# Two-sided attention decode: A's output weights loaded between the two halves of the last A pair's V, and the slots of the last three loads exchanged

## The chip, the cores and the metric

The kernel runs on one core of one Trainium2 chip. The metric is the device time of one execution in microseconds. Before the change it is 831.22 us, the median of 3 runs (830.82 to 831.3). Times in the trace are counted from the start of the profiled execution's span.

## What is computed

Two attention decodes of one token, A and B, with 32 heads of 128 each and no sharing of K and V between heads. Side A looks at all 16384 cached positions, side B at the last 4096. For each side:

```python
q = (x @ wq)                                  # 512 -> 32 heads x 128
scores = einsum("bhqd,bhkd->bhqk", q, k) * (Dh ** -0.5)
p = softmax(scores)
o = einsum("bhqk,bhkd->bhqd", p, v)
out = o.reshape(B, Sq, Hq * Dh) @ wo          # 4096 -> 512
# B: k, v are cut to the last W = 4096 positions
return concatenate([a, b], axis=-1)
```

Nearly all of the data is K and V: 268 MB for A, 67 MB for B. Each of the four weight matrices (A's and B's `wq` and `wo`) has 4096 KB. Every element is read once.

## The kernel before

**Steps.** The work is cut into 20 steps T = 0..19 (lines 88 to 97). Sixteen are pairs of A heads, four are groups of eight B heads (T = 0, 7, 13, 19). So T = 18 is the last A pair, and T = 19 is the last step, B's. Each step has two halves u = 0, 1: for A the two halves of the positions of one pair of heads, for B two groups of four heads. A loop over x = 2T + u (line 400) runs all halves in order, and `tc.manual_schedule()` (line 374) keeps each engine's instructions in the order in which the program writes them.

**A half.** VectorE multiplies the half's K by q (`scores_prod`, L194), adds up over the head dimension in four halvings (`scores_tree`, L201) and one reduction (L207), and takes the maximum (L212). TensorE and VectorE bring the maximum of each head together (L214, L219, L223, L226), ScalarE makes the exponentials and spreads them by head (`soft`, L231 to L253). TensorE multiplies the probabilities with V (`pv`, L275, 32 matmuls of 128x512 for a half). ScalarE scales and evicts (L291), and eight small matmuls (L306) and a copy (L310) turn the result into columns of O.

**What lies one step behind.** V of step T is loaded and multiplied while step T + 1 is scored. At x = 38, the first half of step 19, the program issues `pv(17, 1)`, then the load of V(18, 1), then `pv(18, 0)`. At x = 39 come `pv(18, 1)` and the loads for the end. Here V(T, u) is the half u of step T's V.

**Slots.** K tiles live in a ring of two K slots of 8192 KB each (`kslot`, tag `kring`), V halves and the `wq` matrices in a ring of two V slots of 4096 KB each (`vslot`, tag `vring`). A load into a slot waits until the slot's last readers are done. V(18, 0) and V(19, 0) use one V slot, V(18, 1) and V(19, 1) the other. After step 18's scores, its K slot is free; before the change it takes A's `wo` in one half and B's `wo` in the other (`W`, lines 409 and 424).

**Queue.** All loads of K, V and weights are issued by SyncE, in program order, on one queue. A wait in front of one load holds back all the loads behind it. The order of the loads at the end, before the change: K of step 19 (two halves), V(17, 1), V(18, 0), V(18, 1), V(19, 0), A's `wo`, V(19, 1), B's `wo` in five pieces (16, 8, 4, 2 and 2 of 32 rows per partition).

**The end.** After the loop, TensorE's program order is: the last maximum and sums, `pv(19, 0)` (L275), its columns (L306), A's permutation and output projection (`permute_o` L327 and L332, `project_out_columns` L345, 128 matmuls), the transposition of A's output (L363), then `pv_columns` for V(19, 1) (L317, 128 matmuls), B's permutation, B's output projection (L345, 128 matmuls in five pieces, each of which waits for its piece of B's `wo`), and B's output (L357, L363, L367, store L368).

Of the kernel before, what the change touches and what calls it, by code (L numbers as in the profile page):

```python
# [16 lines left out]
HQ, DH = 32, 128  # L17
CH = 128
# [7 lines left out]
def kernel(  # L26
# [34 lines left out]
    def kslot(name):  # L61
        return kring.tile([P, 2 * CH, DH], BF16, tag="kring", name=name)

    def vslot(name):
        return vring.tile([P, CH, DH], BF16, tag="vring", name=name)
# [7 lines left out]
    A, B = _Side(), _Side()  # L73
# [22 lines left out]
    NT = len(steps)  # L96
    assert na == HQ // 2 and nb == HQ // 8

    K, V = {}, {}

    def b_window(cache, g):
        return cache[0, 4 * g : 4 * g + 4, SkB - WB : SkB, :].rearrange("h (i l) d -> i h (l d)", l=CH)

    def a_pair(cache, g):
        return cache[0, 2 * g : 2 * g + 2, :, :].rearrange("h (i l) d -> (h i) l d", l=2 * CH)

    def new_k(T):
        K[T] = kslot("kt")

    def load_k(T, u=None):  # L110
        s, g = steps[T]
        if s is A:
            nc.sync.dma_start(
                out=K[T][:, :, :].rearrange("p l d -> p (l d)"),
                in_=a_pair(A_k_cache, g).rearrange("p l d -> p (l d)"),
            )
        else:
            for v in (0, 1) if u is None else (u,):
                nc.sync.dma_start(
                    out=K[T][:, v * CH : (v + 1) * CH, :].rearrange("p l d -> p (l d)"),  # L120
                    in_=b_window(B_k_cache, 2 * g + v),
                )

    def load_v(T, u):
        s, g = steps[T]
        V[T, u] = vslot("vt")
        if s is A:
            src = a_pair(A_v_cache, g)[:, u * CH : (u + 1) * CH, :].rearrange("p l d -> p (l d)")
        else:
            src = b_window(B_v_cache, 2 * g + u)  # L130
        nc.sync.dma_start(out=V[T, u][:, :, :].rearrange("p l d -> p (l d)"), in_=src)

    def load_wq(s):
        s.wq_t = vslot("wqt")
        nc.sync.dma_start(
            out=s.wq_t[:, :, :].rearrange("p a b -> p (a b)").rearrange("p (c f) -> p c f", c=KC),
            in_=s.wq.rearrange("(p c) f -> p c f", c=KC),
        )

    def load_wo(s, W, u, pieces):  # L140
        s.wo_t = W[:, u * CH : (u + 1) * CH, :].rearrange("p a b -> p (a b)").rearrange("p (r f) -> p r f", r=HQ)
        src = s.wo.rearrange("(p r) f -> p r f", r=HQ)
        r = 0
        for n in pieces:
            nc.sync.dma_start(out=s.wo_t[:, r : r + n, :], in_=src[:, r : r + n, :])  # L145
            r += n

    def make_masks(s):
        nc.vector.tensor_reduce(out=s.mask[:, :], in_=by_head(s, identf[:, :]), axis=AX.X, op=ALU.add)
        nc.vector.tensor_copy(s.rows[:, :, :], s.mask[:, :].unsqueeze(2).broadcast_to([P, s.nh, 4]))  # L150

    def spread_x(s, flat):
        s.xb = flat[:, 0 : s.nh * KC * P].rearrange("p (h c m) -> p h c m", h=s.nh, c=KC)
        nc.vector.memset(s.xb, 0.0)
        for j in range(s.nh):
            dst = s.xb[:, j, :, :]
            if s is A:
                dst = dst.rearrange("p c (h i) -> p c h i", h=s.nh)[:, :, j, :]
            else:
                dst = dst.rearrange("p c (i h) -> p c i h", h=s.nh)[:, :, :, j]  # L160
            nc.vector.tensor_copy(dst, s.xT[:, :].unsqueeze(2).broadcast_to([P, KC, P // s.nh]))  # L161

    def project_q(s):
        wq = s.wq_t[:, :, :].rearrange("p a b -> p (a b)").rearrange(
            "p (c g h d) -> p c h g d", c=KC, h=s.nh, d=DH
        )
        for g in range(0, HQ // s.nh, 4):
            qp = ps_t.tile([P, 4, DH], F32, tag="tp", name="qp")
            n = KC * s.nh
            for k in range(n):  # L170
                c, j = divmod(k, s.nh)
                nc.tensor.matmul(  # L172
                    qp[:, :, :], lhsT=s.xb[:, j, c, :], rhs=wq[:, c, j, g : g + 4, :],
                    start=(k == 0), stop=(k == n - 1),
                )
            nc.scalar.copy(s.q[:, g : g + 4, :], qp[:, :, :])
# [13 lines left out]
    def scores_prod(T, u):  # L190
        s, g = steps[T]
        k = K[T][:, u * CH : (u + 1) * CH, :]
        j = g if s is A else 2 * g + u
        nc.vector.tensor_tensor(out=k, in0=k, in1=s.q[:, j : j + 1, :].broadcast_to([P, CH, DH]), op=ALU.mult)  # L194
# [63 lines left out]
    def recip(un):  # L258
        un.r = small.tile([P, 4], F32, tag="r", name="r")
        if un.last:  # L260
            nc.vector.reciprocal(un.r[:, 0 : un.s.nh], un.sm[:, 136 : 136 + un.s.nh])
        else:
            nc.vector.reciprocal(un.r[0 : un.rows, 0:1], un.sm[0 : un.rows, 136:137])  # L263
# [35 lines left out]
    def columns():  # L299
        while evicted:  # L300
            un = evicted.pop(0)
            s, n = un.s, un.rows
            oc = ps_s.tile([P, 4], F32, tag="sp", name="oc")
            sel = identf[0:n, 0:n].rearrange("k (h c) -> k c h", c=4)
            for j in range(4):
                nc.tensor.matmul(  # L306
                    oc[:, 0 : s.nh], lhsT=un.osb[0:n, j * P : (j + 1) * P], rhs=sel[:, j, :],
                    start=(j == 0), stop=(j == 3),
                )
            nc.scalar.copy(s.O[:, un.col : un.col + s.nh], oc[:, 0 : s.nh])  # L310
# [62 lines left out]
    wo_pieces = (16, 8, 4, 2, 2)  # L373
    with tc.manual_schedule():
        for s in (B, A):
            nc.scalar.dma_start(out=s.xT[:, :], in_=s.x[0, 0, :].rearrange("(p c) -> p c", c=KC))
        scratch = kslot("scratch")
        new_k(0)
        load_wq(B)
        load_k(0, 0)  # L380
        load_wq(A)
        load_k(0, 1)
        make_identity(nc, identf[:, :])
        nc.vector.memset(one_f[:, :], 1.0)
        nc.vector.memset(ones_col[:, :], 1.0)
        nc.vector.tensor_copy(ident[:, :], identf[:, :])
        spread_x(B, scratch[:, :, :].rearrange("p a b -> p (a b)"))
        for s in (B, A):
            make_masks(s)
        nc.vector.memset(pick[:, :], 0.0)  # L390
        nc.vector.tensor_copy(
            pick[:, 4 : 4 + P].rearrange("h (m k) -> h m k", k=4)[:, :, 0], identf[0:HQ, 0:HQ]
        )
        spread_x(A, one.tile([P, 2 * KC * P], BF16, tag="o4", name="xbA")[:, :])
        project_q(B)
        project_q(A)
        new_k(1)
        load_k(1)
        done = None
        for x in range(2 * NT):  # L400
            T, u = divmod(x, 2)
            if u == 0 and T >= 1:
                load_v(T - 1, 0)
                if T + 1 < NT:
                    new_k(T + 1)
                    load_k(T + 1)
            if x == 2 * NT - 1:
                load_v(T, 0)
                W = kslot("wot")
                load_wo(A, W, 0, (HQ,))  # L410
            columns()
            scores_prod(T, u)
            if done is not None:
                max_all(done)
                soft(done)
            if u == 0 and T >= 1:
                if T >= 2:
                    pv(T - 2, 1)
                load_v(T - 1, 1)
                pv(T - 1, 0)  # L420
            if x == 2 * NT - 1:
                pv(T - 1, 1)
                load_v(T, 1)
                load_wo(B, W, 1, wo_pieces)
            nxt = scores_tree(T, u)
            if done is not None:
                recip(done)
            evict()
            done = nxt
            if done is not None:  # L430
                unit_max(done)
        columns()
        max_all(done)
        soft(done)
        recip(done)
        pv(NT - 1, 0)
        evict()
        columns()
        permute_o(A)
        project_out_columns(A, (HQ,))  # L440
        store_out(A)
        pv_columns(NT - 1, 1)
        permute_o(B)
        project_out_columns(B, wo_pieces)
        store_out(B)
# [30 lines left out]
```

## Time and profile before

| what | before |
| --- | --- |
| median of 3 runs | 831.22 us (830.82 to 831.3) |
| the profiled execution | 831.32 us |
| its span | 829.5 us |
| bytes read | 352.32 MB |
| VectorE busy | 761.0 us, 92% |
| TensorE matmul busy | 395.2 us, 48% |
| ScalarE busy | 67.8 us, 8% |

The span runs from the first to the last instruction of the trace. The rest of the execution's time, 1.8 us, lies around it. "PE" is TensorE's matmuls, "PEld" its weight loads, "DVE" VectorE, "ACT" ScalarE, and "SPq" what SyncE issues on its DMA queue. A row of a view by windows gives a stretch, the busy time and instruction count of each engine in it, the clock that TensorE was granted (1.00 is full speed), the mean busy share of the 16 DMA engines and the rate that they moved. A row of a timeline gives start, duration, engine, line, operation and names, a count, and in brackets how long the engine was idle before it and which event ended that. The time "to landing" of a load runs from its issue to the last event that reports its arrival.

### The profile page before, as it was taken

To read this page: it belongs to the slowest core of one execution; us is meant where nothing else is said; L and a number is where in the kernel's file an instruction comes from. 1 tells how busy PE (TensorE), PEld (TensorE's weight loads), DVE (VectorE), ACT (ScalarE), POOL (GpSimd) and SP (SyncE) were. 2 spreads that over 40 slices of the span, in tenths; PEclk is the share of its full clock that TensorE was granted. 3 is DMA by queue.
4 is the path that set the end of the run, shared out by engine and by line. 5 is a ranking of instruction groups with operands and counts; after the bars stand their busy time and mean duration, and the time that the engine had idled before them with its cause. 6 is when DMAs were issued, how large, how long until landed. Compare 5 with 4: busy or idle time off the path is not lost.

```text
span 829.5 us, 4817 instructions
## 1 busy us (share of the span) xinstructions
PE 395.2 (48%) x2012; PEld 172.7 (21%) x2012; DVE 761.0 (92%) x356; ACT 67.8 (8%) x196; POOL 0.7 (0%) x6
## 2 busy tenths in 40 slices
PE   3514062808163543637081725455362708082885
PEld 1102021303021211213030312122221303030344
DVE  1899999999999999999999999999999999999920
ACT  0111010101000011101010000011010101000120
POOL 0000000000000000000000000000000000000000
PEclk9756566758595867667585958576666758585895
DMA  9999999999999999999999999999999999999797
GB/s 379 430 430 437 433 458 411 453 408 432 435 427 430 437 455 411 450 412 448 416 444 417 440 425 431 450 416 450 416 441 420 444 417 443 425 433 433 331 431 305
DMA packets 10694, 352.64 MB, mean 425 GB/s; under 512 B 1456, under 2 KB 1456, under 8 KB 1840
## 3 DMA queue, kind: packets, MB, share of 16 engines
q1 hardware_dynamic: 10376, 352.33, 98.7%
q8 instruction: 16, 0.26, 0.1%
q10 hardware_dynamic: 296, 0.00, 0.0%
q14 instruction: 6, 0.05, 0.0%
HBM read 352.32 MB, written 0.00 MB: 425 GB/s over the span
## 4 chain that ended last, share of the span: by engine, by line
DVE 79%; DMA 17%; PE 2%; issue 1%; SPq 0%; ACT 0%; DVEq 0%; ACTq 0%
DVE kt L194 36%; DVE kt L201 35%; DMA kt<-in_A_k_cache_dram 10%; DVE sc L207 5%; DMA wot<-in_B_wo_dram 3%; DMA xTA<-in_A_x_dram 3%; PE o L275 2%; DMA vt<-in_A_v_cache_dram 1%; DVE m L212 1%; DVE Mr L223 1%; DVE M L219 0%; SPq L145 0%; DVE r L263 0%; ACT p L234 0%; PE sm L226 0%
## 5 line engine op out<-in xcount | busy, mean ns | idle before, releaser
L201 DVE TENSOR_TENSOR kt<-kt 128x8192 bf16<-128x8192 bf16 (+3 forms) x160 | 344.9, 2156 | 4.7
L275 PE MATMUL o<-vt,pm 128*8 128x512 bf16 (+1 forms) x1248 | 316.3, 420 | 2.5 <-DMA vt<-in_A_v_cache_dram 2.5
L194 DVE TENSOR_TENSOR kt<-kt,qA 128x16384 bf16<-128x16384 bf16 x32 | 277.5, 8672 | 3.0 <-DMA kt<-in_A_k_cache_dram 3.0
L275 PEld LDWEIGHTS <-pm 128*8 128x8 bf16 (+1 forms) x1248 | 116.2, 94 | 192.5 <-issue 65.1
L214 PE MATMUL sm<-identf,m 128*1 128x128 f32 x24 | 8.4, 350 | 196.7 <-DVE m L212 196.7
L226 PE MATMUL sm<-one_f,Mr 1*128 1x1 f32 x48 | 13.1, 340 | 176.7 <-DVE Mr L223 176.7
L194 DVE TENSOR_TENSOR kt<-kt,qB 128x16384 bf16<-128x16384 bf16 x8 | 69.5, 8681 | 0.0
L207 DVE TENSOR_REDUCE sc<-kt 128x128 f32<-128x1024 bf16 x40 | 48.8, 1220 | 2.9
L226 PEld LDWEIGHTS sm<-one_f,Mr 1*128 1x128 f32 x48 | 11.1, 285 | 183.1 <-DVE Mr L223 183.1
L214 PEld LDWEIGHTS sm<-identf,m 128*1 128x1 f32 x24 | 1.9, 79 | 200.1 <-issue 191.3
L231 ACT ACTIVATE bias<-sm 128x1 f32<-128x1 f32 x24 | 4.1, 171 | 386.8 <-PE sm L226 386.6
L291 ACT ACTIVATE o<-o,r 8x512 f32<-8x512 f32 (+1 forms) x23 | 15.6, 678 | 176.5 <-PE o L275 176.5
L306 PE MATMUL oc<-identf,o 8*128 8x2 f32 (+1 forms) x184 | 25.1, 254 | 3.7 <-ACT o L291 3.7
L306 PEld LDWEIGHTS oc<-identf,o 8*128 8x128 f32 (+1 forms) x184 | 23.1, 193 | 12.0 <-issue 6.5
L321 DVE TENSOR_TENSOR OB<-ocol,r 128x4 bf16<-128x4 f32 x1 | 0.2, 161 | 21.3 <-PE ocol L317 21.3
L172 PE MATMUL qp<-wqt,scratch 128*128 128x512 bf16 x32 | 9.1, 455 | 13.8 <-DVE scratch L161 13.8
L253 ACT ACTIVATE pm<-p,maskA 128x256 bf16<-128x256 bf16 x32 | 14.5, 500 | 0.5
L172 PE MATMUL qp<-wqt,xbA 128*128 128x512 bf16 x32 | 9.7, 475 | 10.2 <-DMA wqt<-in_A_wq_dram 10.2
L310 ACT CAST OA<-oc 128x2 bf16<-128x2 f32 x16 | 2.6, 160 | 109.9 <-PE oc L306 109.9
L234 ACT ACTIVATE p<-sc,bias 128x256 bf16<-128x256 f32 (+1 forms) x24 | 11.3, 472 | 0.8
L161 DVE COPY scratch<-xTB 128x128 bf16<-128x128 bf16 x4 | 0.7, 314 | 10.8 <-DMA xTB<-in_B_x_dram 10.8
L253 ACT ACTIVATE pm<-p,maskB 128x128 bf16<-128x128 bf16 x32 | 10.2, 389 | 0.2
(57 smaller groups left out, 81.5 us busy)
## 6 DMA issues: line engine op xcount, KB each, us to landing
vt<-in_A_v_cache_dram SPq DMA_DIRECT2D x32, 4096.0 KB, 26.8
kt<-in_B_k_cache_dram SPq DMA_DIRECT2D x8, 4096.0 KB, 30.6
vt<-in_B_v_cache_dram SPq DMA_DIRECT2D x8, 4096.0 KB, 29.2
wqt<-in_B_wq_dram SPq DMA_DIRECT2D x1, 4096.0 KB, 12.4
wqt<-in_A_wq_dram SPq DMA_DIRECT2D x1, 4096.0 KB, 31.1
wot<-in_A_wo_dram SPq DMA_DIRECT2D x1, 4096.0 KB
wot<-in_B_wo_dram SPq DMA_DIRECT2D x1, 2048.0 KB, 25.7
wot<-in_B_wo_dram SPq DMA_DIRECT2D x1, 1024.0 KB, 27.6
```

Of the source, the lines that this page charges most:

```text
L172: nc.tensor.matmul(qp[:, :, :], lhsT=s.xb[:, j, c, :], rhs=wq[:, c, j, g : g + 4, :], start=(k == 0), stop=(k == n - 1),)
L194: nc.vector.tensor_tensor(out=k, in0=k, in1=s.q[:, j : j + 1, :].broadcast_to([P, CH, DH]), op=ALU.mult)
L201: nc.vector.tensor_tensor(out=k[:, :, 0:w], in0=k[:, :, 0:w], in1=k[:, :, w : 2 * w], op=ALU.add)
L207: nc.vector.tensor_reduce(out=un.sc[:, c0 : c0 + CH], in_=k[:, :, 0:8], axis=AX.X, op=ALU.add)
L212: nc.vector.tensor_reduce(out=m[:, :], in_=un.sc[:, 0 : un.n], axis=AX.X, op=ALU.max)
L214: nc.tensor.transpose(un.sm[0:1, 0:P], m[:, :], identf[:, :])
L226: nc.tensor.matmul(un.sm[:, 128:129], lhsT=Mr[:, :], rhs=one_f[:, :], start=True, stop=True)
L234: nc.scalar.activation(out=p[:, 0 : un.n], in_=un.sc[:, 0 : un.n], func=ACT.Exp, scale=inv, bias=bias[:, :], accum_out=cs[:, :],)
L253: nc.scalar.activation(out=un.pm[:, :, j, :], in_=p[:, 0 : un.n].rearrange("p (i c) -> p i c", c=4), func=ACT.Copy, scale=s.mask[:, j : j ...
L275: nc.tensor.matmul(un.o[0 : un.rows, :], lhsT=un.pm[:, i0 + i, :, :].rearrange("p a b -> p (a b)"), rhs=V[T, u][:, 4 * i : 4 * i + 4, :], ...
L291: nc.scalar.activation(out=un.osb[0 : un.rows, :], in_=un.o[0 : un.rows, :], func=ACT.Copy, scale=un.r[0 : un.rows, 0:1],)
L306: nc.tensor.matmul(oc[:, 0 : s.nh], lhsT=un.osb[0:n, j * P : (j + 1) * P], rhs=sel[:, j, :], start=(j == 0), stop=(j == 3),)
```

## The change

Three edits, all about where and when the last four loads go.

1. A's `wo` is issued one half-step earlier, at x = 38 (2·NT − 2) in place of x = 39. In SyncE's order it now stands between V(18, 0) and V(18, 1), and it still goes into the first half of step 18's K slot.
2. V(19, 1) no longer takes a V slot, but the second half of that K slot, and is issued right behind V(19, 0), ahead of `pv(18, 1)` in the program.
3. B's `wo` takes the V slot that V(19, 1) had, the one that V(18, 1) was in, so its load waits for `pv(18, 1)`. `load_wo` takes a whole slot in place of a slot and a half's number.

The order of the loads after the change: K of step 19, V(17, 1), V(18, 0), A's `wo`, V(18, 1), V(19, 0), V(19, 1), B's `wo` in the same five pieces. The instructions of TensorE, VectorE and ScalarE and their order are the same as before.

```diff
-    def load_v(T, u):
+    def load_v(T, u, dst=None):
         s, g = steps[T]
-        V[T, u] = vslot("vt")
+        V[T, u] = vslot("vt") if dst is None else dst
...
-    def load_wo(s, W, u, pieces):
-        s.wo_t = W[:, u * CH : (u + 1) * CH, :].rearrange("p a b -> p (a b)").rearrange("p (r f) -> p r f", r=HQ)
+    def load_wo(s, W, pieces):
+        s.wo_t = W.rearrange("p a b -> p (a b)").rearrange("p (r f) -> p r f", r=HQ)
...
+            if x == 2 * NT - 2:
+                W = kslot("wot")
+                load_wo(A, W[:, 0:CH, :], (HQ,))
             if x == 2 * NT - 1:
                 load_v(T, 0)
-                W = kslot("wot")
-                load_wo(A, W, 0, (HQ,))
+                load_v(T, 1, W[:, CH : 2 * CH, :])
             columns()
...
             if x == 2 * NT - 1:
                 pv(T - 1, 1)
-                load_v(T, 1)
-                load_wo(B, W, 1, wo_pieces)
+                load_wo(B, vslot("wot")[:, :, :], wo_pieces)
```

## The prediction

> **What bounds the kernel now.** I read the page's bytes first, then the chain that ended last, then the last 60 us by timeline and by windows.
>
> ```profile
> HBM read 352.32 MB, written 0.00 MB: 425 GB/s over the span
> DVE 79%; DMA 17%; PE 2%; issue 1%; SPq 0%; ACT 0%; DVEq 0%; ACTq 0%
> ```
>
> The chain gives VectorE 79%, but the DMA engines show nines in almost all forty slices: the loads are one unbroken stream, and VectorE, 92% busy, keeps up with it. The change touches only the end, so what counts is what limits that stretch. The chain of waits, in order of time, has there:
>
> ```profile
> 763.84 9.46 PE o L275 x32
> 773.31 12.04 DMA vt<-in_A_v_cache_dram
> 785.39 8.98 PE o L275 x32
> ...
> 797.13 28.59 DMA wot<-in_B_wo_dram
> ```
>
> `pv(17, 1)` ends at 773.2 and frees a V slot; only then is V(18, 1) issued (773.31), and it lands 12.04 us later. At the very end the last piece of B's `wo` is what is waited for. Between the two the stream is unbroken. In front of it is a hole, as the windows around 773 show:
>
> ```profile
> 764.00:768.00 4.00, 4.00 (x11) 1.23 (x10) 3.97 (x2) 0.53 (x2) 0.00 (x0) 0.50 0.99 426
> 768.00:772.00 4.00, 4.00 (x18) 1.51 (x17) 3.83 (x5) 0.00 (x0) 0.00 (x0) 0.90 0.53 225
> 772.00:776.00 4.00, 4.00 (x20) 1.62 (x19) 4.00 (x4) 0.68 (x1) 0.00 (x0) 1.00 0.44 131
> 776.00:780.00 4.00, 4.00 (x20) 1.50 (x18) 4.00 (x1) 0.00 (x0) 0.00 (x0) 1.00 1.16 500
> ```
>
> The last column is the rate. Against the mean of 425 GB/s the second window lacks 200 and the third 294 GB/s, the fourth gives 75 back: 419 GB/s over 4 us, 1.7 MB or 3.9 us of the stream. This hole is what A's `wo` can fill. The question is who then sets the end, and for that TensorE's timeline from 785 counts:
>
> ```profile
> 785.39 8.98 PE L275 MATMUL o<-vt,pm 128*8 128x512 bf16 x32 [2.48 <-DMA vt<-in_A_v_cache_dram]
> ...
> 811.92 0.38 PE L363 MATMUL out_rows<-identf,cols 128*4 128x128 f32 x1 [0.25 <-ACT cols L361]
> 815.83 3.57 PE L317 MATMUL ocol<-pm,vt 128*128 128x4 bf16 x128 [3.54 <-DMA vt<-in_B_v_cache_dram]
> ...
> 820.83 1.85 PE L345 MATMUL out_cols<-OpB,wot 128*128 128x1 bf16 x64 [0.27 <-ACT OpB L336]
> 823.23 1.01 PE L345 MATMUL out_cols<-OpB,wot 128*128 128x1 bf16 x32 [0.56 <-DMA wot<-in_B_wo_dram]
> 824.51 1.00 PE L345 MATMUL out_cols<-OpB,wot 128*128 128x1 bf16 x24 [0.26 <-DMA wot<-in_B_wo_dram]
> 825.78 0.38 PE L345 MATMUL out_cols<-OpB,wot 128*128 128x1 bf16 x8 [0.27 <-DMA wot<-in_B_wo_dram]
> ```
>
> The brackets are the point. After `pv(18, 1)` TensorE waits for loads only 3.54 + 0.56 + 0.26 + 0.27 = 4.63 us in all. A second chain, TensorE's, runs that close behind the stream, and it starts when V(18, 1) lands.
>
> **A's wo ahead of V(18, 1).** Its slot is free when step 18's last reduction ends (VectorE, L207, 751.40 + 1.22 = 752.6), so it is issued there, long before the hole, and SyncE is held by nothing new. V(18, 1) is still issued at 773.31, since that waits for `pv(17, 1)`, but now behind A's `wo`.
>
> When does it land? From issue plus time to landing: the second half of step 19's K 714.5 + 39.2 = 753.7, V(17, 1) 735.47 + 27.9 = 763.4, V(18, 0) 742.38 + 30.7 = 773.1. So a full queue lands 4096 KB every 9.7 us, in order of issue. A's `wo` lands at 773.1 + 9.7 = 782.8, and V(18, 1) at **792.5**, which is 7.1 us later than 785.35 now. The hole gives back only 2.6 of the 9.7 us, because a load has landed when its slowest DMA engine is done: the busy share falls from about 768.5 on, but that engine goes on to 773. Bounds: if the lag were not carried on, the stream would follow the engines that end first, 768.5 + 2 × 9.7 = 788 and a little for arrival, so 789; if one engine is held up in this stretch, as between V(19, 0) (780.23 + 15.0 = 795.2) and V(19, 1) (794.41 + 21.4 = 815.8), which took 20.6 us for two loads in place of 19.4, 793.7. I take 792.5; two plain steps of 9.7 are the nearest rows.
>
> One rule can be weighed here. The row first: V(18, 1) into an empty queue took 12.04 us, while loads into a full one took about 28 to 31. The Trainium skill, "DMA: Bandwidth & Descriptors", section "Rules for kernel authors", advises to issue a DMA early and wait late, since the fixed cost then overlaps; its section on the anatomy of a DMA fits about 2.0 us plus bytes over 436 GB/s, 11.6 us here, near the row. By that rule the early `wo` hides some 2 us and the sum would be about 829. By the rows the early load, which nobody needs before 815, stands in an in-order queue ahead of one that TensorE is waiting for.
>
> **pv(18, 1).** It costs 8.98 us now, after a short idle of 2.48; `pv(17, 1)`, after a long one, costs 9.46; `pv(18, 0)`, warm from the start, 6.97. The granted clock is 0.50 at the start of each of the first two, and 1.00 later. It will now start after 9.6 us of idle. The longest cold start nearby: the 64 matmuls from 609.22 took 16.92 us, which less a warm half of 6.97 leaves 9.95. Idle time seems to add little beyond the first microseconds, so I take 9.2, between 8.98 and 9.46, with 7.0 and 10.0 as ends. It ends at 792.5 + 9.2 = 801.7.
>
> **From there to A's output.** The same instructions as now, 794.38 to 812.30, 17.92 us: maximum, sums, `pv(19, 0)`, columns, projection of A. V(19, 0) lands at 802.2, and `pv(19, 0)` would start at 797.85 + 7.3 = 805.2, so it waits for nothing. A's `wo` has long been there. End at 819.6.
>
> **V(19, 1) in the K slot.** It is issued right behind V(19, 0) at about 780.8, since the slot needs no further wait, and lands at 802.2 + 9.7 = 811.9 (now 815.8). Being early is worth nothing: TensorE comes to it at 819.6. So the wait of 3.54 us goes. `pv_columns` takes 3.57 us (granted clock 0.50 already, so it can't get slower by that), and from its end to B's projection are 820.83 - 819.40 = 1.43 us: 824.6.
>
> **B's wo in the V slot.** This adds a wait, for `pv(18, 1)`, until 801.7. Behind it in SyncE's queue is only the last store. The stream has work until 811.9, so the wait is hidden; five issues take 2.62 us. Without that cover it would cost up to the 12 us of a load into an empty queue. Landing: 811.9 + 9.9 (825.7 - 815.8 now) = 821.8, before TensorE comes to it at 824.6. So the waits between pieces go. The 128 matmuls then cost between 3.56 (A's, busy) and 4.24 (B's, busy, 1.85 + 1.01 + 1.00 + 0.38), A's with its gap 3.90; I take 3.8: 828.4 in place of 826.17.
>
> **The sum.** From the last of these matmuls to the end of the span are 829.5 - 826.17 = 3.4 us, unchanged: 831.8, so **+2.3 us**. The same by waits: V(18, 1) +7.15, `pv(18, 1)` +0.2, less 3.54 for V(19, 1), less 5.34 - 3.8 = 1.54 in B's projection: +2.3. The profiled execution took 831.32 us, 0.1 above the median of the runs: 831.3 + 2.3 = **833.6 us**, 0.29% slower. VectorE's work ends at 791.7 either way. What a measurement of this kernel can tell from no change is about 0.2%, 1.7 us.
>
> **Rivals.**
>
> 1. *The stream alone sets the end* (faster). Its last landing moves from 825.7 to 821.8, 3.9 us, giving 827.4. For it: the chain now ends in B's `wo` for 28.59 us. Against it: TensorE's chain has only 4.63 us of waits to give, and V(18, 1) comes 7.1 us later. It decides only where V(18, 1) lands before about 786. 5%.
> 2. *V(18, 1) comes 2 to 3.5 us earlier than I take* (no change): the lag of the slowest engine is made up while A's `wo` runs. Then it lands at 789 to 790.5, and the end is 831.3 + 2.3 - 3.5 to 831.3 + 2.3 - 2 = 830.1 to 831.6. For it: the mean engine is idle for 3.9 us, not 2.6. Against it: three loads in a row landed 9.7 us apart with the lag in place. 22%.
> 3. *TensorE's slow start takes longer* (slower still): `pv(18, 1)` at 10.0 us, and a delayed engine on top, 792.5 + 1.2: 831.3 + 2.3 + 0.8 + 1.2 = 835.6. For it: both have happened in this trace. Against it: not in the same stretch. 6%.
> 4. *The change does not reorder the stream*: A's `wo` is held by some wait until 773. Then V(18, 1) still follows it, with the hole back: landing at 785.35 + 9.7 = 795.1, worse by another 2.6 us, 836.2. Against it: the only reader of the slot is done at 752.6. 1%.
>
> **Numbers.** My forecast of 833.6 has 66%, between 832.9 and 835.5. With the rivals: slower by over 0.2% 0.72, within 0.2% 0.23, faster 0.05. The range of 831.2 to 835.6 takes in the upper part of rival 2 and the ends of the unknown terms, and leaves out rivals 1 and 4 and the lower part of rival 2.
>
> **What would show it.** Right: no hole near 773 in the windows; `pv(18, 1)` starts at about 792.5 on a wait for its V; `pv_columns` follows A's output transposition without a wait for a load; B's projection in one stretch; the chain of waits at the end all TensorE from 792 on. Wrong: `pv(18, 1)` before 790, or any wait for B's `wo` left, or a DMA link at the chain's end.
>
> A second rule stands by itself. The row is the granted clock, 0.50 for the first 3.9 us of `pv(18, 1)` now and for 5.1 us of `pv(17, 1)`. The Trainium skill, "TensorE: Matmul & The Clock Gate", Part 1, says that a cold array runs at half clock until a free-running window of about 3.4 us was busy throughout, so how long depends on where the first matmul falls. By the page `pv(18, 1)` would average 9.5 us and the sum be 833.9; by the rows it is 833.6.

## The result, and the profile after

The changed kernel takes 833.78 us, the median of 8 runs (833.3 to 836.83), against 831.03 of before (830.51 to 831.3) on the same chip. The ratio is 1.0045, with a 95% interval of 1.0029 to 1.0061: slower. The profiled execution took 833.46 us with a span of 831.7.

The eight runs fall into two groups, five from 833.3 to 834.1 and three from 836.7 to 836.8. The profiled execution is of the first group. The second group is taken up in the first experiment.

The windows around the old hole, of the changed kernel (the last column is the rate in GB/s, the one before it the busy share of the DMA engines):

```profile
768.00:772.00 4.00, 4.00 (x17) 1.45 (x15) 3.83 (x4) 0.00 (x0) 0.00 (x0) 0.81 1.01 434
772.00:776.00 4.00, 4.00 (x20) 1.66 (x19) 4.00 (x4) 0.68 (x1) 0.00 (x0) 1.00 1.03 438
```

The hole is gone: 434 and 438 GB/s where 225 and 131 stood. A's `wo` is issued at 752.70 and lands 30.2 us later, at 782.9. The chain of waits, in order of time, shows what that does:

```profile
773.70 18.88 DMA vt<-in_A_v_cache_dram
792.62 9.16 PE o L275 x32
...
805.31 7.02 PE o L275 x32
...
818.52 0.60 issue
...
824.75 3.57 PE out_cols L345 x128
```

V(18, 1) takes 18.88 us from issue to landing in place of 12.04. From there to the end no load appears in the chain any more; before, it ended in 28.59 us of waiting for B's `wo`. TensorE's timeline of the same profile:

```profile
792.62 9.14 PE L275 MATMUL o<-vt,pm 128*8 128x512 bf16 x32 [9.65 <-DMA vt<-in_A_v_cache_dram]
...
819.72 3.60 PE L317 MATMUL ocol<-pm,wot 128*128 128x4 bf16 x128
...
824.75 3.56 PE L345 MATMUL out_cols<-OpB,wot 128*128 128x1 bf16 x128 [0.27 <-ACT OpB L336]
```

One wait has grown from 2.48 to 9.65 us (ahead of `pv(18, 1)`), and those for V(19, 1) and for the pieces of B's `wo`, 4.63 us in all, are gone: `pv_columns` has no bracket, and B's projection is one stretch of 128 where it was four.

### The profile page after: what moved, and what is told of

The parts are those of the page before. It is cut to its first block, busy times and chain, and to the rows that moved or that the text cites. A ratio compares the mean times of both kernels' runs of the same rounds, so it can differ in the third digit from the quotient of the medians.

```text
span 831.7 us, 4818 instructions
## 1 busy us (share of the span) xinstructions
PE 394.2 (47%) x2012; PEld 171.9 (21%) x2012; DVE 761.0 (92%) x356; ACT 67.8 (8%) x196; POOL 0.7 (0%) x6
## 4 chain that ended last, share of the span: by engine, by line
DVE 79%; DMA 15%; PE 5%; issue 1%; ACT 1%; DVEq 0%; ACTq 0%
DVE kt L194 36%; DVE kt L201 35%; DMA kt<-in_A_k_cache_dram 10%; DVE sc L207 5%; PE o L275 3%; DMA xTA<-in_A_x_dram 3%; DMA vt<-in_A_v_cache_dram 2%; PE out_cols L345 1%; DVE m L212 1%; DVE Mr L223 1%; DVE M L219 0%; PE ocol L317 0%; PE oc L306 0%; ACT o L291 0%; DVE r L263 0%
## 5 line engine op out<-in xcount | busy, mean ns | idle before, releaser
L219 DVE TENSOR_REDUCE M<-sm 1x2 f32<-1x128 f32 (+1 forms) x24 | 6.5, 271 | 10.2 <-PE sm L214 10.2
## 6 DMA issues: line engine op xcount, KB each, us to landing
wot<-in_A_wo_dram SPq DMA_DIRECT2D x1, 4096.0 KB, 30.2
```

## The experiments

Each kernel ran in alternation with the kernel before on the same chip. Ratios are against those runs.

### The changed kernel again: what are the two groups?

No edit.

> The changed kernel unaltered. Its eight runs so far lie in two groups, 833.3 to 834.1 (five) and 836.7 to 836.8 (three), while the runs of before stay within 830.5 to 831.3. Theory (TensorE's chain after V(18, 1) sets the end): every run is 2.3 us or more above before, and what scatters is the chain's slow starts. Rival (one DMA engine is held up by up to 3 us in some executions): then before would scatter as much, since its end is a load. A run of the second group, if the profile catches one, shows which term grew: the landing of V(18, 1) (792.6 in the profile of after), pv(18, 1) (9.14) or pv(19, 0) (7.07).

Measured: 836.44 us (833.91 to 836.72, 5 runs), ratio 1.0054 (1.0040 to 1.0068). One run was in the first group, four in the second, and the profile caught one of these (836.41 us, span 834.6). The 24 runs of before spread from 830.13 to 832.07, evenly. TensorE's timeline of this slower execution:

```profile
792.76 9.62 PE L275 MATMUL o<-vt,pm 128*8 128x512 bf16 x32 [9.65 <-DMA vt<-in_A_v_cache_dram]
...
806.05 9.80 PE L275 MATMUL o<-vt,pm 128*16 128x512 bf16 x32
```

V(18, 1) is there at 792.76 in place of 792.62, so it is no load. `pv(18, 1)` costs 0.5 us more, and `pv(19, 0)` 9.80 us in place of 7.07. The windows of the two `pv` and of the stretch between them, first of this execution, then of the faster one of the first profile (the third column from the end is the granted clock):

```profile
792.76:802.38 9.62, 9.62 (x33) 3.26 (x32) 0.00 (x0) 0.00 (x0) 0.00 (x0) 0.73 1.01 436
802.38:806.05 3.67, 1.98 (x13) 1.69 (x13) 0.55 (x2) 2.37 (x9) 0.00 (x0) 0.83 0.99 429
806.05:815.85 9.80, 9.80 (x33) 3.39 (x32) 0.18 (x1) 0.60 (x3) 0.00 (x0) 0.72 0.95 404
```

```profile
792.62:801.76 9.14, 9.14 (x33) 3.17 (x32) 0.00 (x0) 0.00 (x0) 0.00 (x0) 0.77 1.00 430
801.76:805.24 3.48, 1.79 (x14) 1.50 (x14) 0.55 (x2) 2.17 (x8) 0.00 (x0) 1.00 1.03 443
805.24:812.31 7.07, 7.07 (x33) 2.80 (x32) 0.18 (x1) 0.80 (x3) 0.00 (x0) 1.00 0.96 413
```

Between the two `pv` TensorE is busy for about half of 3.5 us. In one execution the clock stays at 1.00 through that, in the other it drops, and the next 32 matmuls pay for it: 0.5 + 0.2 + 2.7 = 3.4 us with the slower sums, less the stall of 0.60 us ("issue" in the first profile's chain) that is absent here, comes close to the 2.9 between the spans.

### TensorE kept busy ahead of pv(18, 1)

```diff
             if x == 2 * NT - 1:
+                wm = ps_t.tile([16, 512], F32, tag="tp", name="wm")
+                for i in range(32):
+                    nc.tensor.matmul(
+                        wm[:, :], lhsT=ident[:, 0:16], rhs=A.q[:, 0:4, :], start=(i == 0), stop=(i == 31)
+                    )
                 pv(T - 1, 1)
```

> The changed kernel with 32 more matmuls of 16x512 on constant operands, written to a PSUM tile that nobody reads, put on TensorE just ahead of pv(18, 1), where it is idle for 9.65 us. They keep TensorE busy until V(18, 1) lands. Theory (the chain from V(18, 1)'s landing sets the end, and a slow start is one of its terms): V(18, 1) lands at 792.6 as before, pv(18, 1) falls from 9.14 to about 7.0, span 831.7 - 2.1 = 829.6, time about 831.3. If the group near 836.7 comes from slow starts in pv(18, 1), it disappears here. Rival (the end is set by the stream): no change, 833.5.

Measured: 833.53 us (831.76 to 833.64, 8 runs), ratio 1.0022 (1.0012 to 1.0032). TensorE's timeline of a run of 833.64:

```profile
792.39 7.07 PE L275 MATMUL o<-vt,pm 128*8 128x512 bf16 x32 [1.25 <-DMA vt<-in_A_v_cache_dram]
...
803.13 8.51 PE L275 MATMUL o<-vt,pm 128*16 128x512 bf16 x32
...
818.34 2.67 PE L317 MATMUL ocol<-pm,wot 128*128 128x4 bf16 x93
822.35 1.07 PE L317 MATMUL ocol<-pm,wot 128*128 128x4 bf16 x35 [1.34 <-issue]
```

`pv(18, 1)` costs 7.07 us, as expected, and the group near 836.7 is gone. Two runs only (831.76 and 832.0) come near the expected 831.3; the other six lie at 833.5 to 833.6. In the one of these that was profiled, the clock drops ahead of `pv(19, 0)` instead (8.51 us), and a stall of 1.34 us appears in `pv_columns`, after 93 of 128 matmuls, on nothing but "issue" (time in which the engine waits for nothing that the profile shows).

### The extra matmuls in the gap as well

```diff
+        fill(3)
         columns()
         max_all(done)
+        fill(5)
         soft(done)
```

`fill(n)` is the block of the last experiment with n matmuls; `fill(32)` stays ahead of `pv(18, 1)`.

> The changed kernel with the 32 extra matmuls ahead of pv(18, 1) and eight more between pv(18, 1) and pv(19, 0) (three ahead of the columns, five ahead of the sums), all into a PSUM tile that nobody reads. Theory (the two groups of runs differ by the clock in pv(19, 0), which drops in some executions since TensorE does little in the 3.7 us between the two): pv(18, 1) and pv(19, 0) both take about 7.1 us, and the runs are one group near 831.8 to 832.3, since at most 0.3 us of the extra matmuls is on the path. Rival (the groups come from the loads): two groups remain, about 3 us apart.

Measured: 832.24 us (831.77 to 833.63, 11 runs), ratio 1.0016 (1.0007 to 1.0025). Nine runs lie within 831.8 and 832.5, two at 833.6. The profile:

```profile
792.41 7.07 PE L275 MATMUL o<-vt,pm 128*8 128x512 bf16 x32 [1.04 <-DMA vt<-in_A_v_cache_dram]
...
803.06 7.07 PE L275 MATMUL o<-vt,pm 128*16 128x512 bf16 x32
...
816.87 2.45 PE L317 MATMUL ocol<-pm,wot 128*128 128x4 bf16 x85
820.30 1.28 PE L317 MATMUL ocol<-pm,wot 128*128 128x4 bf16 x43 [0.98 <-issue]
```

Both `pv` run at full clock, and the groups 3 us apart are gone. So the two groups are TensorE's clock. Even with both `pv` at full clock in the profile, the median is 1.0 us behind the runs of before (831.27); the profiled run (831.86) has a stall of 0.98 us in `pv_columns`. What the two runs at 833.6 are was not profiled.

### Half and a quarter of A's wo ahead

```diff
-                load_wo(A, W[:, 0:CH, :], (HQ,))
+                load_wo(A, W[:, 0:CH, :], (16,))
             if x == 2 * NT - 1:
                 load_v(T, 0)
+                load_wo(A, W[:, 0:CH, :], (HQ - 16,), 16)
                 load_v(T, 1, W[:, CH : 2 * CH, :])
```

The last argument is the first row. For the quarter it is 8 in place of 16.

> The changed kernel, but only half of A's wo (2048 KB) goes ahead of V(18, 1); the other half is issued behind V(19, 0). Slots as in the changed kernel. Theory (V(18, 1) is late by what stands ahead of it, less the 2.6 us of hole): V(18, 1) lands at 773.1 + 4.9 + 9.7 = 787.7, TensorE's chain then ends 4.9 us sooner than in the changed kernel, span 826.9, unless the stream ends it: its last landing is 821.8 in either case, which gives 825.6. So span about 827, time about 828.7, 2.4 us under before. Rival (the new slots and the wait of B's wo cost the time): as slow as the changed kernel, 833.5.

> As the kernel with half of A's wo ahead, but with a quarter (1024 KB). Theory: V(18, 1) lands at 773.1 + 2.4 + 9.7 = 785.2, as in before, so TensorE's chain is not late at all; the hole is nearly filled, and the stream ends at about 821.8 in place of 825.7, which sets the end: span about 825.7, time 827.4, 3.8 us under before (0.45%). Rival (filling the hole is worth nothing, since TensorE or VectorE bounds the end anyway): 831.

Measured: half 832.09 us (830.37 to 832.59, 11 runs), ratio 1.0006 (0.9997 to 1.0014); a quarter 831.05 us (829.32 to 832.99, 11 runs), ratio 0.9996 (0.9986 to 1.0005). TensorE's timeline with half of it ahead, and then with a quarter (lines of the program are one lower here: L274 is `pv`, L344 the projections, L316 `pv_columns`):

```profile
787.74 9.80 PE L274 MATMUL o<-vt,pm 128*8 128x512 bf16 x32 [4.83 <-DMA vt<-in_A_v_cache_dram]
...
801.22 9.89 PE L274 MATMUL o<-vt,pm 128*16 128x512 bf16 x32
```

```profile
785.10 8.75 PE L274 MATMUL o<-vt,pm 128*8 128x512 bf16 x32 [2.46 <-DMA vt<-in_A_v_cache_dram]
...
807.24 3.38 PE L344 MATMUL out_cols<-OpA,wot 128*128 128x1 bf16 x126 [0.28 <-ACT OpA L335]
812.22 0.19 PE L344 MATMUL out_cols<-OpA,wot 128*128 128x1 bf16 x2 [1.59 <-issue]
...
813.02 3.49 PE L316 MATMUL ocol<-pm,wot 128*128 128x4 bf16 x125
818.96 0.22 PE L316 MATMUL ocol<-pm,wot 128*128 128x4 bf16 x3 [2.45 <-issue]
```

The landings are as expected, 787.7 and 785.1: V(18, 1) is late by what stands ahead of it. The times are not. With half of it ahead, both `pv` run with the clock down (9.80 and 9.89), 0.7 and 2.8 us more than in the first group of the changed kernel: 3.5 of the 3.8 us by which the profile's span of 830.7 exceeds the expected 826.9. With a quarter ahead, in a run of 829.4, TensorE stands still for 1.59 + 2.45 = 4.0 us in its small matmuls, on no event of another engine. The first stall costs nothing at the end: V(19, 1) lands only at 813.0 (issued at 781.21, 31.8 us to landing), and `pv_columns` starts then. The second does cost: `pv_columns` ends at 819.2, where 816.6 would have been possible. The run is 2.0 us above the expected 827.4, its span 1.9 above the expected 825.7. B's `wo` landed at 822.9 (795.72 + 27.2) in place of 821.8; with the 3.8 us that lie between the last landing and the end of the span in the profile of before, the stream alone would have ended the span at 826.7. By this estimate the later landing makes 1.0 of the 1.9 us and the second stall 0.9. What the slower runs of this kernel, up to 832.99, spent was not profiled. The theory of V(18, 1) holds, but the clock and, with a quarter, the stall and a later end of the stream were missing behind it.

### What is TensorE waiting for?

The two stalls come after 126 matmuls of A's projection and after 125 of `pv_columns`. Counted from the start of the program, these are the 1749th and the 1877th weight load, 128 apart, 256 instructions with their matmuls. With 32 matmuls inserted ahead the second stall came after 93, with 40 after 85: the place moves by the number inserted, so it is fixed in TensorE's instruction stream and not in the data. In all the profiles such a stall ended 1.2 to 1.6 us after one of the 16 fetches on the profile's instruction queue (0.26 MB in all, 16 KB each) had ended. To see whether such a fetch is held up by the loads:

```diff
-                load_wo(B, vslot("wot")[:, :, :], wo_pieces)
+                B.wo_t = A.wo_t
```

in the kernel with a quarter ahead. So the load of B's `wo` is left out, and B's projection reads A's.

> The kernel with a quarter of A's wo ahead, without the load of B's wo: B's projection is computed with A's wo, so this part of the work is left out. The stream then ends with V(19, 1) at about 812.5. It looks at TensorE's stalls at its 1749th and 1877th weight load (256 instructions apart), which each ended 1.2 to 1.6 us after a fetch on the instruction queue. Theory (the fetch waits behind queued loads on its DMA engine): the fetch for the second one, which started 6.0 us after TensorE reached the first with the loads of wo in the queue, now starts within 2 us of the stream's end or of its cause, and the stall in pv_columns, 2.45 us, falls under 1 us. Rival (a fetch is late whatever the queue holds): 2 us or more remain.

Measured: one run of 827.07 us. TensorE's timeline:

```profile
812.88 0.19 PE L344 MATMUL out_cols<-OpA,wot 128*128 128x1 bf16 x2 [1.40 <-issue]
...
813.60 3.58 PE L316 MATMUL ocol<-pm,wot 128*128 128x4 bf16 x128
```

The first stall, while V(19, 1) still arrives, is there (1.40). The second is gone. In the trace the fetch for it starts 1.05 us after the first stall's end, and 4.3 us after it in the kernel with B's `wo` in the queue. So a fetch is late while loads are queued, and two bursts of 128 small matmuls in a row run out of instructions meanwhile. This is one run of each, but the other profiles agree. Where the stream has at least 3.9 us to go when TensorE passes the place of the first stall (before, half, a quarter, and the three kernels of the next two sections), the next fetch starts 2.2 to 4.7 us later; where it has at most 2.4 us to go (this kernel and both profiles of the changed one), about 1.1 us later, and there is no second stall. In the profile of before the fetch was 4.1 us late as well, but TensorE spent that time waiting for V(19, 1).

### The slots alone, and the order alone

The slots and waits of the changed kernel with the old order of loads:

```diff
             if x == 2 * NT - 2:
                 W = kslot("wot")
-                load_wo(A, W[:, 0:CH, :], (HQ,))
             if x == 2 * NT - 1:
                 load_v(T, 0)
+                load_wo(A, W[:, 0:CH, :], (HQ,))
                 load_v(T, 1, W[:, CH : 2 * CH, :])
```

> The changed kernel's slots and waits (V(19, 1) in the K slot without a wait, B's wo behind pv(18, 1)), but A's wo issued at x = 39 behind V(19, 0), so that the order of the loads is that of before. Theory (only the place of A's wo in the stream costs): V(18, 1) lands at 785.4 again, the stream keeps its hole, the last landing stays at 825.7, time 831.1, no change against before. Rival (the new slots, or the wait of B's wo, cost the time): about 833.5 or more.

Measured: 831.38 us (830.48 to 831.8, 11 runs), ratio 1.0000 (0.9992 to 1.0009). TensorE's timeline shows the picture of before:

```profile
784.68 8.65 PE L275 MATMUL o<-vt,pm 128*8 128x512 bf16 x32 [1.70 <-DMA vt<-in_A_v_cache_dram]
...
815.15 3.58 PE L317 MATMUL ocol<-pm,wot 128*128 128x4 bf16 x128 [3.52 <-DMA wot<-in_B_v_cache_dram]
```

The other half, A's `wo` early and the slots of before:

```diff
                 load_v(T, 0)
-                load_v(T, 1, W[:, CH : 2 * CH, :])
...
                 pv(T - 1, 1)
-                load_wo(B, vslot("wot")[:, :, :], wo_pieces)
+                load_v(T, 1)
+                load_wo(B, W[:, CH : 2 * CH, :], wo_pieces)
```

> Edit 1 alone: A's wo at x = 38 between the halves of the last A pair's V, with the slots of before (V(19, 1) in a V slot behind pv(18, 1), B's wo in the second half of the K slot). Theory (the place of A's wo costs it all): V(18, 1) lands at 792.6, TensorE's chain is that of the changed kernel; V(19, 1), issued at about 802 with the stream nearly drained, lands at about 814, B's wo at about 824, both just ahead of TensorE. Time as the changed kernel, 833.4, with runs near 836.5 where the clock drops in pv(19, 0). Rival (the new slots take part in the loss): under 832.5.

Measured: 837.29 us (835.42 to 837.65, 5 runs), ratio 1.0071 (1.0057 to 1.0085). TensorE's timeline of the run of 835.42:

```profile
792.56 8.37 PE L275 MATMUL o<-vt,pm 128*8 128x512 bf16 x32 [9.71 <-DMA vt<-in_A_v_cache_dram]
...
820.30 3.52 PE L317 MATMUL ocol<-pm,vt 128*128 128x4 bf16 x125
825.06 0.22 PE L317 MATMUL ocol<-pm,vt 128*128 128x4 bf16 x3 [1.25 <-issue]
```

The order makes the whole loss, and perhaps more than it (the intervals of the two ratios overlap). V(18, 1) lands at the same 792.6, but V(19, 1) is issued only at 801.0, so the stream runs low again (255 GB/s from 800.9 to 804.4), and B's `wo` is still in the queue while TensorE works on `pv_columns` and waits for instructions (1.25 us; none there in the changed kernel's two profiles). In this run the expected 833.4 was too low mainly by that and by a `pv(19, 0)` of 8.76; the four slower runs, 836.74 to 837.65, were not profiled. So the new slots are worth nothing by themselves; that they give back a part of what the new order costs fits these profiles, but is not settled by them.

### The hole filled with what TensorE waits for

```diff
             if x == 2 * NT - 2:
                 W = kslot("wot")
-                load_wo(A, W[:, 0:CH, :], (HQ,))
+                load_v(T - 1, 1, W[:, 0:CH, :])
+                load_v(T, 0, W[:, CH : 2 * CH, :])
             if x == 2 * NT - 1:
-                load_v(T, 0)
-                load_v(T, 1, W[:, CH : 2 * CH, :])
+                load_wo(A, vslot("wot")[:, :, :], (HQ,))
+                load_v(T, 1)
...
-                load_v(T - 1, 1)
+                if T < NT - 1:
+                    load_v(T - 1, 1)
                 pv(T - 1, 0)
...
-                load_wo(B, vslot("wot")[:, :, :], wo_pieces)
             nxt = scores_tree(T, u)
+            if x == 2 * NT - 1:
+                load_wo(B, K[T][:, 0:CH, :], wo_pieces)
```

> The hole is filled by the load that TensorE waits for: V(18, 1) and V(19, 0) go into the two halves of the freed K slot and are issued at 752.6, without a wait for pv(17, 1). A's wo and V(19, 1) take the V slots as these come free, B's wo the first half of step 19's K slot. Theory (who is late is decided by the order in the stream): V(18, 1) lands at 782.8 in place of 785.4 before and 792.6 in the changed kernel, the stream ends at about 821.9 in place of 825.7, and TensorE's chain starts 2.4 us earlier than in before. If the stream ends it, span 825.7 and time 827.5. TensorE's chain can take that away again: pv(19, 0) at half clock costs 2.7 us (seen in the slower profile of the changed kernel), and waits for its own instructions up to 4 us (seen with a quarter of wo ahead). Its slack here is 2 us ahead of V(19, 1) and some 4 ahead of the last piece of wo, so I expect 827.5 to 830, median near 828.5. Rival (the early loads collide with VectorE's or TensorE's work, or the hole is not what costs): 831.

Measured: 828.34 us (827.92 to 829.79, 5 runs), ratio 0.9968 (0.9955 to 0.9980): faster than before, and 5.4 us under the changed kernel's 833.78, which comes from another set of runs (by the ratios, 0.9968 against 1.0045). TensorE's timeline of the run of 828.34:

```profile
783.00 8.75 PE L275 MATMUL o<-wot,pm 128*8 128x512 bf16 x32
...
812.15 3.49 PE L317 MATMUL ocol<-pm,vt 128*128 128x4 bf16 x125 [1.68 <-DMA vt<-in_B_v_cache_dram]
...
822.49 0.37 PE L345 MATMUL out_cols<-OpB,kt 128*128 128x1 bf16 x8 [0.67 <-DMA kt<-in_B_wo_dram]
```

The first line has no bracket: V(18, 1) lands at 783.0 (752.66 + 30.3), just as TensorE ends the work before it, and `pv(18, 1)` does not wait. The waits for loads stand at the end again, at 822.5 in place of 825.8. The stream ends the kernel, 3.3 us sooner.

## Why the prediction was right

Step by step, predicted against the profile of the changed kernel (first group):

| step | predicted | measured |
| --- | --- | --- |
| A's `wo` issued, landed | 752.6, 782.8 | 752.7, 782.9 |
| V(18, 1) lands | 792.5 | 792.6 |
| `pv(18, 1)` | 9.2 us | 9.14 us |
| from its end to A's output | 17.92 us | 18.2 us (801.76 to 819.93) |
| B's projection starts | 824.6 | 824.75 |
| B's projection | 3.8 us | 3.56 us |
| span | 831.8 | 831.7 |
| time | 833.6 us | 833.78 us (median) |

**The sum holds** because it followed who is late, not how many bytes are idle. The stream did gain nearly what rival 1 gave it: the last piece of B's `wo` landed at 822.0 (803.60 + 18.4) in place of 825.7. But TensorE came to that piece only after 824.75, so the stream had ceased to be what ends last. That V(18, 1) is late by the load ahead less 2.6 us is shown at three sizes: 785.1, 787.7 and 792.6 with a quarter, half and all of A's `wo` ahead. That these 2.6 us are the hole of the slowest DMA engine is argued from the landings; no view shows one engine alone. Rival 2 (the lag is made up) is out: V(18, 0) landed at 741.45 + 31.7 = 773.2, A's `wo` at 782.9 and V(18, 1) at 792.6, 9.7 us apart. The rule that the prediction weighed, that an early load hides its fixed cost, would have given about 829; its 11.6 us come from a fit that the section it names states for DMAs issued by GpSimd, while these loads are issued by SyncE. No term of the sum rests on it.

**Two things were luck.** A's output came 0.25 us later than the sum had it and B's projection was 0.24 us shorter, so the two cancel. And five of the first eight runs fell into the lower group; in the second set four of five fell into the upper one, and its median is 836.44, above the range.

**One step was wrong in size**: "The same instructions as now, 794.38 to 812.30, 17.92 us". I took `pv(19, 0)` as 7.07 us because it was so before. In the slower profile the stretch is 802.38 to 822.87, 20.5 us, since the clock drops ahead of `pv(19, 0)`, which then costs 9.80. Seven of the 13 runs of the changed kernel were in that group, at 836.4 to 836.8, above the range. Before, the wait of 3.54 us behind it would have covered such a drop of 2.7 us; the profile of before has none. Rival 3 had the slow start in `pv(18, 1)` alone, with an upper end of 10.0, and the kind of cost was right, but a second one further down the chain was not thought of.

**Not seen at all** were the stalls for instructions. The trace of before has one, 0.34 us, inside the 17.92 (A's projection, 126 + 2 matmuls), and the prediction carried it along as "its gap" without asking what it was. In the changed kernel they stay at 0.60 and less, so the forecast was not hurt. My expectations for half and a quarter of `wo`, worked out by the same sum, missed the medians by 3.4 and 3.7 us. In the profile of half that is the clock; in that of a quarter, a run only 2.0 us above, it is a stall and a later landing in about equal parts.

## What to carry to other kernels

A hole in a stream of loads is worth its length only if what fills it isn't put ahead of something that an engine is waiting for: a queue is served in order, so the load to move into the hole is the one whose landing starts the next chain, here V(18, 1) itself and not weights that are needed 20 us later. When waits for loads are removed from the end of a chain, the chain's own scatter, which the waits had covered, becomes the kernel's. Here that was a clock that can drop in a gap of 3.5 us (up to 2.8 us in `pv(19, 0)`) and instruction fetches behind a full queue (a stall of up to 2.45 us).

## What the hardware showed that was not expected

**The clock can drop without an idle stretch.** TensorE was busy for 1.98 of 3.67 us between the two `pv`, no pause was longer than 1.2 us, and the clock fell in one execution and stayed at 1.00 in another with 1.79 of 3.48. The Trainium skill, "TensorE: Matmul & The Clock Gate", Part 1, says that the throttle returns after an idle window of about 3.4 us and that the window is free-running. The traces' records of the clock fit a free-running window: in each of the eleven profiles the changes in the last 100 us lie whole multiples of 3.41 us apart (797.95, 804.78, 811.61 and 818.43 in the slower profile). What they add is that the window need not be idle: of the 3.41 us up to the drop around this gap, TensorE was busy for 1.7 to 2.5 in the four profiles with one. The matmuls of the two `pv` filled 0.2 to 1.1 us of that; in the six profiles where the clock held and the gap had no extra matmuls, they filled at least 1.35 us of every such window. So where the windows happen to lie over the gap seems to decide; no run tests that.

**Instructions come in by DMA, and late behind loads.** Stalls of 0.2 to 2.5 us on "issue" stand 256 TensorE instructions apart in the bursts of small matmuls at 27 ns each. The Trainium skill, "Runtime: NRT & Kernel Launch", section "Instruction fetch mechanics", gives the same block of 256 instructions and calls the crossing mostly hidden. With loads queued and 128 small matmuls with their weight loads, 256 instructions, in about 3.5 us it isn't: 1.59 and 2.45 us in one execution, of which an estimated 0.9 us reached the end of the kernel.
